# Rearranging the first two batches of a fused attention and MLP kernel: heads on partition halves, spare banks, and a new order of loads

## The chip, the core and the metric

The kernel runs on one core of one Trainium2 chip. The time is that of one launch on the device, in microseconds (us): the median of repeated runs. A second number, the span, is read from a profiled execution, from its first to its last instruction. Five engines matter: TensorE (matrix products; PE in the tables), ScalarE (ACT), VectorE (DVE), GpSimd (POOL), and SyncE (SP), which here issues most of the transfers (DMA). Matrix products write to PSUM, which this kernel divides into eight banks of 512 fp32 columns.

## What is computed

```python
def _attn_ref(q, k, v):                      # each (8 batches, 8 heads, 576 tokens, 64)
    window, dilation, scale = 32, 4, 1.0 / np.sqrt(64)
    scores = scale * np.matmul(q, k.transpose(0, 1, 3, 2))
    rel = pos[:, None] - pos[None, :]
    mask_plain = (rel >= 0) & (rel < window)
    mask_dil = (rel >= 0) & (rel < window * dilation) & (rel % dilation == 0)
    # heads 0 to 3 take mask_plain, heads 4 to 7 take mask_dil
    ...                                      # masked softmax over the keys
    return np.matmul(attn, v)

x = attn_out.transpose(0, 2, 1, 3).reshape(4608, 512)
h = x @ w_in                                 # (512, 2048)
out = np.maximum(0.01 * h, h) @ w_out        # (2048, 512)
```

All inputs and the output are fp32 in DRAM; the kernel computes in fp16 with fp32 sums.

## The kernel before

A small planner in the Python source orders every instruction of every engine before the program is emitted. Priorities (`prio`) and the tables `WHEN`, `FIRST` and `RANKS` steer it; the engines then run their lists strictly in that order.

**The first two batches.** The q and k of batches 0 and 1 (`b < EARLY`) are loaded in rows of 1 KB and turned by TensorE; batches 2 to 7 come later in another way. In each batch a visit `hp` takes two heads: visits 2 and 3 the dilated heads, 0 and 1 the plain ones. Part 0 of a visit has units 0 and 1, part 1 has unit 2, which needs the last 64 tokens ("rest").

```python
FIRST = "bbii0iiicicooii1oooooo"     # order of loads: b, c = q, k, v of batch 0, 1
                                     # i, o = 512 KB of w_in, w_out; 0, 1 = rest of a batch
def heads_of(vi):
    return 4 * (vi // 2) + vi % 2, 4 * (vi // 2) + vi % 2 + 2
...
# load_group: v of the dilated heads, twice with an overlap
lv = [load("SP", at(vs, 0, 128, i * 256, [512, 4], [1, 256]),
           dram(v, base + i * 64 * D, [4 * D, 128], [HS, 4], [1, 256]), 512, 1024, ...)
      for i in range(2)]
...
# load_rest: eight transfers of 16 partitions each
for vi in (2, 3, 0, 1):
    for o, src in ((0, q), (1, k)):
        p0 = 32 * vi + 16 * o
        lo.append(load("SP", at(st, p0, p0 + 16, 0, [256, 2], [1, 256]), ..., 32, 1024, ...))
```

**One unit.** TensorE adds a mask and the scores into one PSUM bank; ScalarE takes the exponential; TensorE multiplies by v. Beside the 64 columns of v lie 64 columns of ones, so that rows 64 to 127 of the result hold the sum of the weights. ScalarE makes the reciprocal as exp(-ln), and VectorE multiplies.

```python
sps = [bank("sps0")]                          # one bank for scores
ops = [bank(f"ops{i}") for i in range(2)]     # two for the weighted values
hps = [bank(f"hps{i}") for i in range(2)]     # two for the MLP's first product
fps = [bank(f"fps{i}") for i in range(2)]     # two for its second; fps[1] also turns k
...
nc.tensor.matmul(st[:, 0:384], ident, bias, start=True, stop=False)            # mask
nc.tensor.matmul(st[:, 192 * i:192 * i + 192], ka, qa, ...)                    # scores, x2
nc.scalar.activation(out=et, in_=st[:, 0:384], func=AF.Exp, scale=SCALE)
for hh in range(2):
    nc.tensor.matmul(ot[:, c:c + 96], va, et[:, c:c + 96], start=True, stop=True)  # x4, 128 columns of v and ones
nc.scalar.activation(out=rt, in_=ot[64:128, 0:384], func=AF.Ln)
nc.scalar.activation(out=rt, in_=rt, func=AF.Exp, scale=-1.0)
nc.vector.tensor_tensor(out=at(xt[m % 2], ...), in0=at(ot, 0, 64, ...), in1=at(rt, 0, 64, ...), op=ALU.mult)
```

**The MLP.** The 4608 tokens make 12 chunks of 384: three for each pair of batches. Chunk 0 is the first 384 tokens of batch 0, chunk 1 those of batch 1, chunk 2 the rest of both.

```python
def up(c, j, ...):        # 16 per chunk: four matmuls of 384 columns, then ACT into gt
    nc.tensor.matmul(ht[:, 0:n], w_in[:, ...j...], at(xt[m % 2], ...), start=(i == 0), stop=(i == NI - 1))
    nc.scalar.activation(out=gt[...], in_=ht[:, 0:n], func=AF.Prelu, alpha=0.01)

def down(c, tt, ...):     # 12 per chunk (3 tt of 4 parts): four matmuls of 512 columns
    nc.tensor.matmul(ft, g[:, ...j...], w_out[:, j * DM:j * DM + DM], start=(j == 0), stop=(j == NJ - 1))
```

Part p of a `down` needs w_out's blocks 4p to 4p+3, that is two of the eight transfers marked `o` in `FIRST`; an `up` needs two of the eight marked `i`.

Of the kernel before, what the change touches and what calls it, by code (L numbers as in the profile page):

```python
# [14 lines left out]
WIN = 32  # L15
AHEAD, LATE = 5.0, 4.0
WHEN = (-5.0, 15.0, 50.0, 77.0, 112.0, 138.0, 172.0, 200.0)
FIRST = "bbii0iiicicooii1oooooo"
RANKS = ((-100.0, 1.0), (-50.0, 1.0), (-40.0, 1.0), (5.0, 1.0))


def _constants():

    ident = np.eye(128, dtype=np.float16)
    p = np.arange(128)[:, None]
    key = p - 32
    c = np.arange(96)[None, :]
    qry = 4 * (c % 24) + c // 24
    rel = qry - key
    band = (rel >= 0) & (rel < WIN)  # L30
    first = band & (key >= 0)
    rel0 = c - p
    d0 = (rel0 >= 0) & (rel0 < WIN)
    c1 = np.arange(48)[None, :]
    rel1 = 96 + c1 - (16 + p)
    d1 = (rel1 >= 0) & (rel1 < WIN)
    masks = np.concatenate([first, band, band, d0, d1], axis=1)
    parts = [ident, masks, np.where(masks, 0.0, -60000.0)]
    return np.concatenate([x.astype(np.float16) for x in parts], axis=1)
# [94 lines left out]
def kernel(  # L134
# [23 lines left out]
    EARLY = 2  # L158

# [19 lines left out]
    NMASK = 288 + 96 + 48  # L179
# [3 lines left out]
    M_PL, M_D0, M_D1 = 128, 128 + 288, 128 + 288 + 96  # L183
# [12 lines left out]
    rc = [sbuf(f"rc{i}", [64, 384], FP32) for i in range(NR)]  # L196
# [3 lines left out]
    rest = sbuf("rest", [128, 512])  # L200
# [5 lines left out]
    sps = [bank("sps0")]  # L206
    ops = [bank(f"ops{i}") for i in range(2)]
    hps = [bank(f"hps{i}") for i in range(2)]
    fps = [bank(f"fps{i}") for i in range(2)]
# [7 lines left out]
    def took(n, size):  # L217
        for a, ta, b, tb in ((4, 9.0, 128, 15.0), (128, 15.0, 256, 20.0), (256, 20.0, 1024, 52.0),
                             (1024, 52.0, 2048, 92.0)):
# [4 lines left out]
    def load(queue, dst, src, n, size, deps, prio):  # L224
# [3 lines left out]
                        LATE if prio > -1478 else 0.0)  # L228
# [27 lines left out]
    for i in range(NT):  # L256
        p = (-2000 if i == 0 else -1900) + i
        t_zero[i] = ([clear("DVE", qbd[i][64:128, 0:S], 0.34, 0.0, p),
                      clear("DVE", qbd[i][0:64, S:2 * S], 0.34, 0.0, p)],
                     [clear("DVE", kt[i][:, 0:PAD], 0.1, 0.0, p)])  # L260
    t_ones = {}
    for i in range(NV):
        p = -1950 if i == 0 else -700
# [7 lines left out]
    kept = {}  # L271

    def heads_of(vi):
        return 4 * (vi // 2) + vi % 2, 4 * (vi // 2) + vi % 2 + 2

    def load_group(b, g, prio):
# [7 lines left out]
        for o, src in ((0, q), (1, k)):  # L284
# [3 lines left out]
            if first:  # L288
                lo = [load(queue, at(st, 0, 128, j * 256, [512, 2], [1, 256]),
                           dram(src, base + j * HS, [4 * D, 128], [2 * HS, 2], [1, 256]),  # L290
# [15 lines left out]
        if dil:  # L306
            lv = [load("SP", at(vs, 0, 128, i * 256, [512, 4], [1, 256]),
                       dram(v, base + i * 64 * D, [4 * D, 128], [HS, 4], [1, 256]),
                       512, 1024, v_old, prio) for i in range(2)]
        elif b == 0:  # L310
            lv = [load("SP", at(vs, PAD, 128, 0, [1, D]), dram(v, 0, [D, 96], [1, D]),
                       96, 256, v_old, prio),
                  load("SP", at(vs, 0, 128, D, [D, 23], [1, D]),
                       dram(v, 64 * D, [D, 128], [96 * D, 23], [1, D]),
                       2944, 256, v_old, prio), t_vz]
        else:
            lv = [load("SP", at(vs, 0, 128, 0, [D, 24], [1, D]),
                       dram(v, base - 32 * D, [D, 128], [96 * D, 24], [1, D]),
                       3072, 256, v_old, prio)]

        for j in range(2):
            nn, n_old = ring("NAT", NNAT, n_users := [])
            na, c_qk = nat[nn], []
            for o in range(2):
                st, s_users = stage[o]
                if early:
                    dst = at(na, 0, 128, o * 512, [D, 2], [128, 4], [1, D])
                    src = at(st, 0, 128, j * 256, [512, 2], [D, 4], [1, D])
# [9 lines left out]
            if not dil:  # L338
                c_v = [cast(at(vt, 0, 128, 0, [768, 2], [128, 6], [1, D]),
                            at(vs, 0, 128, j * 384, [768, 2], [D, 6], [1, D]), 768,  # L340
                            lv + d_old, prio)]
            elif early:
                c_v = [cast(at(vt, 0, 128, i * 512, [1024, 2], [128, 4], [1, D]),
                            at(vs, 0, 128, j * 512 + i * 256, [1024, 2], [D, 4], [1, D]), 512,
                            lv[i:i + 1] + d_old, prio) for i in range(2)]
            else:
                c_v = [cast(at(vt, 0, 128, 0, [1024, 2], [128, 8], [1, D]),
                            at(vs, 0, 128, j * 512, [1024, 2], [D, 8], [1, D]), 1024,
                            lv + d_old, prio)]
            v_users += c_v  # L350
            kept[b, 2 * g + j] = vt, d_users, c_v[1:]
            if early:
                c_v = c_v[:1]
            visits[b, 2 * g + j, 0] = (na, c_qk, n_users, vt,
                                       c_v + [t_ones["d" if dil else "p", dn]], d_users)

    def load_rest(b, prio):

        _, r_old = ring("REST", 1, r_users := [])
        sn, s_old = ring("STG", NST, s_users := [])  # L360
        st, lo = stg[sn], []
        for vi in (2, 3, 0, 1):
            for o, src in ((0, q), (1, k)):
                p0 = 32 * vi + 16 * o
                lo.append(load("SP", at(st, p0, p0 + 16, 0, [256, 2], [1, 256]),
                               dram(src, (b * H + heads_of(vi)[0]) * HS + 512 * D,
                                    [4 * D, 16], [2 * HS, 2], [1, 256]),
                               32, 1024, s_old, prio))
        c = cast(at(rest, 0, 128, 0, [D, 2], [128, 4], [1, D]),
                 at(st, 0, 128, 0, [256, 2], [D, 4], [1, D]), 512, lo + r_old, prio, CENG)  # L370
        s_users.append(c)
        for vi in range(NP):
            vt, d_users, c_v = kept[b, vi]
# [4 lines left out]
    def load_w(n, prio):  # L378
# [15 lines left out]
        for i in range(2):  # L394
            c = cast(dst[i], st[:, i * 512:i * 512 + 512], 512, [t], prio, WENG)
# [7 lines left out]
    WENG = ("POOL", "DVE")  # L403
# [17 lines left out]
    def pieces(b, dil, u):  # L421

        m, res = b // 2, []
        u_lo, u_hi = ((0, 96) if u < 2 else (96, 144)) if dil else (48 * u, 48 * u + 48)
        for u0, nu, base in segs[b]:
# [5 lines left out]
            if dil and u < 2:  # L431
                res.append((key, base + 2 * u * nu + lo - u0, [[nu, 2], [1152, 2], [1, n]], 0,
                            [[192, 2], [96, 2], [1, n]]))
            elif dil:
                res.append((key, base + lo - u0, [[nu, 4], [1152, 2], [1, n]], 0,
                            [[96, 4], [48, 2], [1, n]]))
            else:
                res += [(key, base + 1152 * hh + lo - u0, [[24, 2], [nu, 4], [1, 24]], 96 * hh,
                         [[192, 2], [24, 4], [1, 24]]) for hh in range(2)]
# [7 lines left out]
    def move(dst, src, n, deps, prio):  # L447

        def fn(e):
            if e == "ACT":  # L450
                nc.scalar.copy(out=dst, in_=src)  # L451
            else:
                nc.vector.tensor_copy(out=dst, in_=src)  # L453
        return add((("DVE", 0.1 + n * 0.00065), ("ACT", 0.06 + n * 0.00085)), None, 0.2, deps, fn,
                   prio)

    slot_of, turned_rest = {}, {}

# [7 lines left out]
    def turn(b, hp, part, prio):  # L466
# [30 lines left out]
        def turn_in(bank, src, c):  # L497
            def pe(e):
                for s in range(4):
# [4 lines left out]
        def q_to(i, lo, hi, deps):  # L504
# [5 lines left out]
            else:  # L510
                o, od, id_ = 360 + lo, [[24, 4], [1, n]], [[128, 4], [1, n]]
            return [move(at(qb, 64 * hh, 64 * hh + 64, hh * S + o, *od),
                         at(tpb, 64 * hh, 64 * hh + 64, i, *id_), 4 * n, deps + old + zq, prio)
                    for hh in range(2)]

        def k_to(bank, i, lo, hi, deps):
            n = hi - lo
            if dil:
                o, od = lo, [[144, 4], [1, n]]
            else:  # L520
                o, od = PAD + 4 * lo, [[1, 4], [4, n]]
            return [move(at(kb, 0, 128, o, *od), at(bank, 0, 128, i, [128, 4], [1, n]), 4 * n,
                         deps + old + zk, prio)]

        if part == 1:
            if hp == 2:
                _, q_old = ring("TP", 1, q_users := [])
                tq = add("PE", 0.23, 0.25, c_qk + [t_con] + q_old, turn_in(tpb, na, 0), prio, 0.2)
# [3 lines left out]
            new = (q_to(32 * hp, 128, 144, [tq]) + k_to(tpb, 32 * hp + 16, 128, 144, [tq]))  # L532
            q_users += new
            ev += new
        else:
# [3 lines left out]
            for lo, hi in ((0, 128),) if dil else ((0, 120), (120, 128)):  # L539
                q_users += q_to(lo, lo, hi, [tq])  # L540
            _, k_old = ring("TPK", 1, k_users := [])
            tk = add("PE", 0.23, 0.25, [c_qk[1], t_con] + k_old, turn_in(tpk, na, 512), prio, 0.2)
# [285 lines left out]
```

The softmax here doesn't subtract the row's maximum and nothing guards it: scores larger than these inputs give would overflow.

## Time and profile before

| | |
|---|---|
| time, median of 3 runs | 329.41 us (329.33 to 329.97) |
| span of the profiled execution | 328.3 us |
| TensorE busy | 307.8 us, 94% |
| ScalarE busy | 234.1 us, 71% |
| VectorE busy | 173.6 us, 53% |
| GpSimd busy | 115.4 us, 35% |
| moved by DMA | 52.04 MB, mean 158 GB/s |

Busy shares are averages over stages. A `down` is in the profile a group `fps<-w_out,gt`, an `up` a group `hps<-xt,w_in`. "xN" counts instructions; four make one `up` or one `down`. In tables of instructions in order of time the first number is the start, the second the length.

### The profile page before, as it was taken

Reading aid. Unit: us, or ns where it says so; the run is one execution under the profiler, and the core shown is the slowest. Engines: PE = TensorE matmul, PEld = TensorE weight load, DVE = VectorE, ACT = ScalarE, POOL = GpSimd, SP = SyncE. Lnnn points to the kernel's source line nnn. Section 1 sums busy time; section 2 is a strip of 40 time slices with the busy share of each in tenths; the row PEclk is TensorE's granted clock in tenths of the full one; section 3 lists DMA queues with packets and bytes.
Section 4 is the critical chain, followed back from the end, with each engine's and each line's share of the span. In section 5 each row is a group of like instructions: output and inputs, shape, how many; then the busy total and the mean of one; then the engine's idle time right before and its main releaser. Section 6 shows DMA issues by size and latency. Waiting matters only on the chain.

```text
span 328.3 us, 6295 instructions
## 1 busy us (share of the span) xinstructions
PE 307.8 (94%) x2238; PEld 182.3 (56%) x2238; DVE 173.6 (53%) x382; ACT 234.1 (71%) x520; POOL 115.4 (35%) x166
## 2 busy tenths in 40 slices
PE   6666988999999999999999999999999999999994
PEld 3444654556667656565555555555555555555541
DVE  7455677443777586976865867666343411000011
ACT  2787997854989799699988888887788853334300
POOL 6524443227445371772744736456000000000000
PEclk9997999999999999999999999999999999999998
DMA  8979989999999999999999999996111111111113
GB/s 241 293 239 349 301 271 310 180 228 143 214 151 219 181 156 210 143 212 202 164 189 158 235 193 150 212 166 138 32 34 32 35 32 34 47 50 34 32 32 96
DMA packets 160831, 52.04 MB, mean 158 GB/s; under 512 B 139168, under 2 KB 152096, under 8 KB 160800
## 3 DMA queue, kind: packets, MB, share of 16 engines
q1 hardware_dynamic: 160112, 50.86, 75.3%
q10 hardware_dynamic: 688, 0.78, 1.0%
q8 instruction: 17, 0.28, 0.4%
q14 instruction: 14, 0.11, 0.2%
HBM read 42.19 MB, written 9.44 MB: 157 GB/s over the span
## 4 chain that ended last, share of the span: by engine, by line
PE 78%; ACT 12%; DVE 5%; issue 3%; DVEq 0%
PE fps L706 36%; PE hps L666 34%; PE sps L592 3%; PE ops L631 3%; ACT rc L639 3%; ACT ee L598 3%; ACT gt L673 2%; ACT rc L642 2%; ACT qbd L451 1%; DVE qbd L241 1%; ACT kt L451 1%; DVE qbd L453 1%; DVE kt L453 1%; PE ops L621 1%; PE sps L573 1%
## 5 line engine op out<-in xcount | busy, mean ns | idle before, releaser
L666 PE MATMUL hps<-xt,w_in 128*128 128x384 f16 (+1 forms) x832 | 153.4, 315 | 1.8 <-ACT gt L673 1.2
L706 PE MATMUL fps<-w_out,gt 128*128 128x512 f16 x576 | 146.0, 379 | 0.0
L673 ACT ACTIVATE gt<-hps 128x384 f16<-128x384 f32 (+1 forms) x208 | 95.3, 464 | 50.2 <-PE hps L666 48.2
L666 PEld LDWEIGHTS <-w_in 128*128 128x128 f16 x832 | 76.4, 98 | 45.7 <-issue 2.6
L647 DVE TENSOR_TENSOR xt<-ops,rc 64x192 f16<-64x192 f32 (+1 forms) x144 | 56.1, 411 | 48.9 <-ACT rc L642 48.1
L706 PEld LDWEIGHTS <-gt 128*128 128x128 f16 x576 | 54.5, 98 | 46.7 <-issue 0.4
L715 DVE COPY osb<-fps 128x512 f32<-128x512 f32 x36 | 24.7, 685 | 60.1 <-PE fps L706 59.0
L487 POOL COPY qbd<-turned 64x576 f16<-64x576 f16 x48 | 34.1, 710 | 59.6 <-DVE turned L482 51.4
L598 ACT ACTIVATE ee<-sps 128x384 f16<-128x384 f32 x96 | 46.8, 488 | 9.4 <-PE sps L592 7.6
L639 ACT ACTIVATE rc<-ops 64x384 f32<-64x384 f32 x96 | 46.7, 487 | 8.9 <-PE ops L631 5.0
L612 DVE TENSOR_TENSOR ee<-ee,con 128x384 f16<-128x384 f16 x72 | 35.4, 492 | 29.0 <-ACT ee L598 28.3
L642 ACT ACTIVATE rc<-rc 64x384 f32<-64x384 f32 x96 | 49.6, 518 | 1.6
L237 POOL CAST nat<-stg 128x576 f16<-128x576 f32 (+1 forms) x55 | 36.0, 678 | 23.8 <-DMA stg<-in_q_dram 15.6
L592 PE MATMUL sps<-qbd,kt 128*128 128x192 f16 x160 | 26.5, 247 | 1.4 <-ACT kt L451 0.7
L592 PEld LDWEIGHTS <-kt 128*128 128x128 f16 x160 | 16.0, 103 | 19.6 <-issue 7.2
L493 DVE STREAM_TRANSPOSE kt<-nat 128x576 f16<-128x576 f16 x24 | 18.0, 763 | 3.7 <-POOL nat L237 3.5
L482 DVE STREAM_TRANSPOSE turned<-nat 128x576 f16<-128x576 f16 x24 | 18.0, 762 | 0.1
L631 PEld LDWEIGHTS <-vp 128*128 128x128 f16 x192 | 12.9, 98 | 8.8 <-issue 2.0
L237 POOL CAST vd<-vst 128x1024 f16<-128x1024 f32 (+1 forms) x20 | 17.0, 881 | 1.9 <-DMA vst<-in_v_dram 1.7
L631 PE MATMUL ops<-ee,vp 128*128 128x96 f16 x192 | 15.9, 206 | 1.1 <-DVE xt L647 1.0
L237 POOL CAST vp<-vst 128x768 f16<-128x768 f32 x16 | 13.4, 862 | 6.6 <-DMA vst<-in_v_dram 6.3
L573 PE MATMUL sps<-con 128*128 128x384 f16 x24 | 7.9, 331 | 6.1 <-ACT ee L598 5.9
(49 smaller groups left out, 130.1 us busy)
## 6 DMA issues: line engine op xcount, KB each, us to landing
vst<-in_v_dram SPq DMA_DIRECT2D x16, 512.0 KB, 6.2
stg<-in_q_dram SPq DMA_DIRECT2D x48, 144.0 KB, 4.8
stg<-in_k_dram SPq DMA_DIRECT2D x48, 144.0 KB, 4.3
vst<-in_v_dram SPq DMA_DIRECT2D x7, 768.0 KB, 6.8
out_dram<-osb SPq DMA_DIRECT2D x16, 192.0 KB, 2.9
gt<-in_moe_w_in_dram SPq DMA_DIRECT2D x5, 512.0 KB, 6.8
out_dram<-osb SPq DMA_DIRECT2D x24, 96.0 KB, 2.1
out_dram<-osb SPq DMA_DIRECT2D x16, 128.0 KB, 2.9
```

The lines of the kernel that those rows point to most:

```text
L237: ENG[e].tensor_copy(out=dst, in_=src)
L487: lambda e, p0=p0, hh=hh: nc.gpsimd.tensor_copy(out=at(qb, p0, p0 + 64, hh * S + o, *od), in_=at(xb, p0, p0 + 64, i, *id_)), prio)
L592: nc.tensor.matmul(st[:, 192 * i:192 * i + 192], ka, qa, start=not by_pe, stop=i == 1 or not by_pe)
L598: lambda e: nc.scalar.activation(out=et, in_=st[:, 0:384], func=AF.Exp, scale=SCALE), prio + 0.1)
L612: ENG[e].tensor_tensor(out=io, in0=io, in1=mk, op=ALU.mult)
L631: nc.tensor.matmul(ot[:, c:c + 96], va, et[:, c:c + 96], start=True, stop=True)
L639: lambda e: nc.scalar.activation(out=rt, in_=ot[64:128, 0:384], func=AF.Ln),
L642: lambda e: nc.scalar.activation(out=rt, in_=rt, func=AF.Exp, scale=-1.0),
L647: nc.vector.tensor_tensor(out=at(xt[m % 2], h0 % 2 * 64, h0 % 2 * 64 + 64, h0 // 2 * 1152 + x, *o_), in0=at(ot, 0, 64, c, *i_), in1=at(rt, ...
L666: nc.tensor.matmul(ht[:, 0:n], w_in[:, i * DFF + j * 128:i * DFF + j * 128 + 128], at(xt[m % 2], 0, 128, i * 1152 + x0 + x, [1, n]), start ...
L673: lambda e: nc.scalar.activation(out=gt[c % NG][:, j * n_c + x:j * n_c + x + n], in_=ht[:, 0:n], func=AF.Prelu, alpha=0.01),
L706: nc.tensor.matmul(ft, g[:, j * n_c + tt * 128:j * n_c + tt * 128 + 128], w_out[:, j * DM:j * DM + DM], start=(j == 0), stop=(j == NJ - 1))
```

## The change

It touches batches 0 and 1 only, and the order of the loads.

- A unit's two heads now lie next to each other in the model's width, and their weighted values are written to partitions 0 to 63 and 64 to 127 of one bank, by matmuls of 64 columns; two more matmuls with a tile of ones write the sums beside them. Ln, Exp and the final product then work on 128 partitions by 192 columns, where it was 64 by 384.
- In batch 0's part 0, before the MLP needs them, one `hps` bank serves as a second bank for scores and the other as a third for weighted values.
- The last 64 tokens of q and k come in two transfers of 128 partitions, where it was eight of 16. The dilated v is loaded once; its last 64 tokens follow in a small transfer.
- The turned k is copied out with a contiguous destination; in batch 1, q and k are turned into one bank. Most of these copies are now VectorE's alone.
- The loads come in a new order, with weights ahead of most of batch 1, and v apart from q and k.

```diff
-FIRST = "bbii0iiicicooii1oooooo"
-RANKS = ((-100.0, 1.0), (-50.0, 1.0), (-40.0, 1.0), (5.0, 1.0))
+FIRST = "ibvbv0iiooiicioiicyoooooy1"          # v, y: v of batch 0, 1
+RANKS = ((-40.0, 2.0), (5.0, 0.5), (-40.0, 1.0), (40.0, 3.0))
...
-    sps = [bank("sps0")]
+    banks = {"S": [bank("sps0")], "O": ops}
+    banks["S0"] = banks["S"] + hps[1:]
+    banks["O0"] = ops + hps[:1]
...
+    return (2 * vi, 2 * vi + 1) if b < EARLY else (4 * (vi // 2) + vi % 2, ...)
...
+        if dil and early:
+            lv = [load("SP", at(vs, 0, 128, 0, [256, 4], [1, 256]),
+                       dram(v, base, [4 * D, 128], [HS, 4], [1, 256]), 512, 1024, v_old, prio_v)]
...
+        for o, src in ((0, q), (1, k)):
+            lo.append(load("SP", at(st, 0, 128, o * 256, [1, 256]),
+                           dram(src, b * H * HS + 512 * D, [HS, 8], [4 * D, 16], [1, 256]),
+                           128, 1024, s_old, prio))
+        lv = load("SP", at(vs, 0, 16, 1024, [256, 4], [1, 256]), ..., 64, 1024, v_old, prio)
...
-                o, od = PAD + 4 * lo, [[1, 4], [4, n]]                         # k_to
+                o, od, id_ = PAD + 4 * lo, [[4, n], [1, 4]], [[1, n], [128, 4]]
...
+            if tiled:                                                          # values
+                for x in range(5 if small else 3):
+                    for hh in range(2):
+                        p0 = 64 * hh
+                        if x == (4 if small else 2):
+                            nc.tensor.matmul(ot[p0:p0 + 64, 192:384], ones, ...)
+                        ...
+                            nc.tensor.matmul(ot[p0:p0 + 64, 96 * x:96 * x + 96],
+                                at(vt, 0, 128, (...) * 128, [1, D]), et[...], ...)
...
+        if tiled:
+            r_in, r_out, n_r = ot[:, 192:384], rt[:, 0:192], 192
...
-                down(n_c, tt, acts, gt_free[n_c])
+                end = tt * 128 + 128
+                down(n_c, tt, [[t for t, x in a if x < end] for a in acts], gt_free[n_c])
```

Matmuls on idle data that keep TensorE busy in the gaps are put in by the planner up to the first `down`, before and after.

## The prediction

> **What bounds the kernel now.** I read the stages first: busy time in five stretches of the span. The columns are the stretch, its length, then busy time and instructions of PE, PEld, DVE, ACT and POOL, the granted TensorE clock, the DMA share and GB/s.
>
> ```profile
> 0.00:30.00 30.00, 18.86 (x166) 11.93 (x167) 16.82 (x58) 20.15 (x44) 14.36 (x26) 0.99 0.95 273
> 30.00:57.75 27.75, 24.09 (x200) 15.09 (x198) 19.31 (x48) 24.45 (x57) 11.70 (x18) 0.95 0.98 301
> 57.75:75.00 17.25, 17.25 (x121) 9.85 (x120) 7.32 (x17) 11.89 (x26) 5.25 (x8) 1.00 1.08 195
> 75.00:323.50 248.50, 247.64 (x1756) 145.38 (x1754) 129.52 (x260) 177.57 (x395) 84.05 (x116) 1.00 0.71 128
> ```
>
> From 57.75 us to the last product at 323.5 us TensorE is busy for 264.9 of 265.75 us. What happens there can't be shortened by making another engine faster. Before 57.75 us it is another kernel: the DMA share is 0.95 to 0.98, and TensorE's busy time holds waits, fillers and a slow clock. So the question is how much of the MLP is done when the packed part begins. TensorE's instructions in order of time show it:
>
> ```profile
> 29.99 1.49 PE L666 MATMUL hps<-xt,w_in 128*128 128x384 f16 x4
> ...
> 50.55 1.13 PE L706 MATMUL fps<-w_out,gt 128*128 128x512 f16 x4
> ...
> 57.75 1.46 PE L666 MATMUL hps<-xt,w_in 128*128 128x384 f16 x8 [0.99 <-ACT gt L673]
> ```
>
> The first up runs at 30 us, the first down at 50.6, and the up at 57.75 is the first of chunk 1. By the order of instructions, 16 ups and 2 downs lie before it; 10 downs of chunk 0 are still owed. Why so late, GpSimd's list tells, since its casts start when data lands (the bracket is the idle time before, and what ended it):
>
> ```profile
> 16.72 1.60 POOL L237 CAST vp<-vst 128x768 f16<-128x768 f32 x2 [2.76 <-DMA vst<-in_v_dram]
> 19.59 0.61 POOL L237 CAST w_in<-gt 128x512 f16<-128x512 f32 x1 [1.26 <-DMA gt<-in_moe_w_in_dram]
> 24.68 0.61 POOL L237 CAST w_in<-wst 128x512 f16<-128x512 f32 x1 [4.49 <-DMA wst<-in_moe_w_in_dram]
> ...
> 36.78 0.61 POOL L237 CAST nat<-stg 128x512 f16<-128x512 f32 x1 [0.98 <-DMA stg<-in_q_dram]
> ...
> 42.03 1.79 POOL L237 CAST vp<-vst 128x768 f16<-128x768 f32 x2 [3.03 <-DMA vst<-in_v_dram]
> ...
> 61.90 0.67 POOL L237 CAST w_out<-xt 128x512 f16<-128x512 f32 x1 [1.90 <-DMA xt<-in_moe_w_out_dram]
> ```
>
> The last weights land at 61.9 us, so chunk 0 can't be finished before. The rates of the transfers over the first 75 us, in 40 slices of 1.875 us, say whether the memory was at its limit:
>
> ```profile
> GB/s 7 187 382 348 348 348 311 218 274 388 115 121 283 357 310 377 351 364 359 334 235 239 378 318 369 90 54 368 380 342 334 286 89 149 138 139 113 308 359 151
> ```
>
> Some 350 GB/s is the usual rate; the dips to 115 and 121 (20 to 24 us) and to 90 and 54 (47 to 51 us) are the sixteen small rest transfers. Inside the early units ScalarE is the engine that is waited for:
>
> ```profile
> PE sps L573 <- ACT ee L598: 5.9, 9, 1.2
> ```
>
> ```profile
> L642 ACT ACTIVATE rc<-rc 64x384 f32<-64x384 f32 x24 | 12.3, 517 | 0.2
> L639 ACT ACTIVATE rc<-ops 64x384 f32<-64x384 f32 x24 | 11.6, 486 | 1.2 <-PE ops L631 0.6
> ```
>
> Nine times the single score bank waited for the exponential, 5.9 us in all; Ln and Exp of the sums take about 1.0 us for each of 24 units.
>
> **What the Trainium skill says.** "ScalarE: Activation LUTs", section "What ACT_TABLE_LOAD costs", gives 186 ns + 0.833 ns per element for an activation with immediates: 506 ns for 384 columns, where the trace has 486 and 517. For 192 columns it gives an estimate of 346 ns. "DMA: Bandwidth & Descriptors", section "Measured (HBM→SBUF, 128 partitions, SWDGE, issued from GpSimd)", calls transfers under 64 KB dominated by their descriptors; the eight of 32 KB here agree (worked out below). "TensorEngine Tiling (Array Packing)", sections "Key Properties" and "Restrictions", says that column tiles can work at once, that a change of mode drains the array, and that tiling turns off the fast weight load; nothing in this trace shows any of it. "TensorE: Matmul & The Clock Gate", "Part 1", says that an idle window of about 3.4 us halves the clock. The trace agrees: the first up, after a stretch of fillers and waits, takes 1.49 us where later ones are 0.65 apart.
>
> **The parts.** *Tiled units.* ScalarE loses 2 x (0.50 - 0.35) = 0.3 us a unit, 24 units: 7 us. VectorE: 128x192 once (0.35, as 64x192 has now) in place of 0.55 or of two at 0.34: about 6 us in all. TensorE: four products of 96 columns and two of 192 are 768 columns where it was 384; at 0.163 us for 384 (a quarter of an up) that is +0.16 us a unit or +4 us in all if nothing runs side by side, but nearly all of it before the packed part. *Spare banks.* They serve 8 of 24 units and can take up to some 4 of the 5.9 us of waits. *Contiguous k.* The plain k copies cost 1.2 to 1.3 us against 0.41 for the dilated; I expect 0.4 to 0.7, four times. These three make batch 0 ready sooner: its first up should run at 23 to 25 us in place of 30. None of them shortens the end by itself, since weights land later than that.
>
> *Loads.* This is the part that counts. Eight transfers of 512 KB between 24.68 and 36.78 us give 1.51 us each. The plain v, 768 KB in rows of 256 bytes, took 42.03 - 36.78 - 1.51 = 3.7 us. The eight rest transfers and one of weights took 24.68 - 19.59 = 5.1, so the rest took 3.6 us for 256 KB. In the new kernel a first w_in (+512 KB) and a dilated v loaded once (-512 KB) cancel out: batch 0's plain v lands at 16.7 again. The rest, two transfers of 128 KB and one of 64 KB, I take as 1.1 us: 17.8. Twenty transfers of 512 KB follow in the list before batch 1's plain v. I find no buffer in their waits that isn't long free, so at 1.51 us: the last w_in, the 12th, at 35.9; the last w_out, the 20th, at 48.0 (61.9 before); batch 1's plain v at 51.7 (42.0 before); its rest at 52.5 to 52.8.
>
> *TensorE's new order.* Before the first up of chunk 1 stand 16 ups and 12 downs: all of chunk 0. After the last w_out only some six downs and the units are left, 6 x 0.865 = 5.2 us, which fits into 48.6 to 54. What decides then is batch 1's tail: rest q, k at 52.5, cast of twice the columns 1.0, turning 0.7, two final products 0.35 each and four copies of 0.19 on VectorE 1.5 with a handover of 0.2, mask and scores 0.6, exponential 0.75, values 0.7, all with their handovers: 58.0 us for chunk 1's first up, as late as before.
>
> *Sum.* The packed part was 265.75 us with 10 downs owed; without them it is 265.75 - 10 x 0.865 = 257.1. The units left then are a little fewer (-0.5). The span is 58.0 + 257.1 - 0.5 + the end after the last product, 4.8 = 319.4. I add 1.0 for a slow clock or holes, because fillers now end with the first down at about 31 us while TensorE still waits for w_out between 36 and 48. The median lies 329.41 - 328.3 = 1.1 above the span: 321.5 us.
>
> **Rivals.** *(a) Loads run as now planned but less densely:* a wait on a buffer, or GpSimd behind (it casts alone all of w_in, 16 x 0.61 us, and the turned inputs wait in its list), moves everything after it. Against: 14 casts between 25.6 and 39 us are only 8.5 us. Each microsecond is one in the result; 3 us late gives 324.5. *(b) The array suffers:* mode changes around the 64-column products and slow clock from 36 us on. If each tiled unit cost 0.3 us more than I count, the 12 of batch 1 give 3.6 us, partly in waiting time: 323 to 325. *(c) ScalarE becomes the limit in chunk 1,* since ups now come without the downs of chunk 0 between them and only two `hps` banks hold them: 16 activations of 0.47 and about 4.5 us of units are 12 us against some 15 us of TensorE. So I expect no hole, or 1 us. Likewise batch 2 is needed some 8 us sooner; its loads start about as before, at 53, and its first scores come near 75, so 2 us at most. *(d) Only the unit's shortening counts, and the loads were hidden:* then downs would still come late, and the time stays at 327 to 329. Against it stands the DMA share of 0.95 to 0.98. *(e) Better:* the units of batch 1 finish faster than my chain, at 55 to 56: 318 to 319.5.
>
> **Range and chances.** The memory sets a floor near 52 us for batch 1, so the gain hardly passes 11 us; (a) and (b) pull the other way, one at a time some 3 us, seldom both. I put eight tenths in 317.5 to 327.0. Two per cent faster is 322.8, just above my number: 0.62; within 2%, 0.33; slower, 0.05, for a stall that the order doesn't show.
>
> **What would show it.** Right: the last w_out cast starts near 48, the plain v of batch 1 is cast near 52, no dip for the rest, first up at 23 to 25, first down near 31, all 12 downs of chunk 0 before the up of chunk 1 at 57 to 59, and TensorE full from there on. Ln and Exp near 350 ns. Wrong: the up of chunk 1 after 60, holes of several us in TensorE after it, or values products far above 0.33 us a unit.

## The result, and the profile after

| | before | after |
|---|---|---|
| time, median | 329.69 us (329.33 to 330.18) | 320.99 us (320.75 to 322.0) |
| ratio | | 0.974, 95% interval 0.9715 to 0.9767 |
| span of the profiled execution | 328.3 us | 319.4 us |
| first up of chunk 0 | 29.99 us | 24.56 us |
| first up of chunk 1 | 57.75 us, two downs done | 58.14 us, all twelve done |
| last w_out cast by GpSimd | 61.90 us | 47.09 us |

The kernel is 8.7 us faster. The busy time by stretch of the kernel after, with the columns as in the prediction (the last stretch ends at the last product, 314.5 us):

```profile
0.00:30.00 30.00, 23.72 (x217) 14.78 (x218) 20.71 (x73) 15.97 (x41) 17.14 (x32) 0.94 0.97 308
30.00:57.75 27.75, 25.35 (x212) 14.44 (x210) 19.11 (x54) 14.45 (x39) 14.99 (x21) 1.00 1.00 301
57.75:75.00 17.25, 17.19 (x132) 10.34 (x133) 5.08 (x13) 11.32 (x28) 7.40 (x10) 1.00 1.07 217
75.00:314.50 239.50, 239.06 (x1714) 140.96 (x1711) 124.88 (x257) 174.63 (x393) 78.83 (x108) 1.00 0.58 123
```

TensorE is full from 57.75 us on, as it was before. ScalarE has lost 14.2 us of busy time in the first 57.75 (20.15 + 24.45 before, 15.97 + 14.45 now). TensorE's instructions in order of time, for the first up, the first down, and the first up of chunk 1 with what stands just before it:

```profile
24.56 0.33 PE L741 MATMUL hps<-xt,w_in 128*128 128x384 f16 x1
...
32.30 1.04 PE L782 MATMUL fps<-w_out,gt 128*128 128x512 f16 x4
...
57.81 0.31 PE L678 MATMUL ops<-ee,vd 128*64 128x48 f16 x8 [1.56 <-DVE xt L722]
57.93 0.28 PE L672 MATMUL ops<-ee,ones 128*64 128x192 f16 x2
58.14 1.47 PE L741 MATMUL hps<-xt,w_in 128*128 128x384 f16 x8
```

GpSimd's casts show when the last weights and batch 1's plain v land:

```profile
47.09 0.62 POOL L243 CAST w_out<-xt 128x512 f16<-128x512 f32 x1 [0.57 <-DMA xt<-in_moe_w_out_dram]
...
49.63 0.83 POOL L243 CAST vp<-vst 128x768 f16<-128x768 f32 x1 [1.92 <-DMA vst<-in_v_dram]
```

And the rate of the transfers over the first 75 us, in slices of 1.875 us:

```profile
GB/s 3 227 278 383 385 385 327 287 245 211 252 364 403 376 399 403 404 381 381 384 401 407 398 360 306 120 189 166 244 178 168 169 230 387 214 77 182 195 240 266
```

Where the rests are loaded (15 to 21 us, 50 to 54 us) the rate falls to 211 and 166, no longer to 115 and 54. The one slice of 120 lies at 47 to 49 us, ahead of the rest. The groups of the early units, by shape (count, busy us, mean ns, idle time before):

```profile
L718 ACT ACTIVATE rc<-rc 128x192 f32<-128x192 f32 x23 | 7.7, 365 | 0.3
L722 DVE TENSOR_TENSOR xt<-ops,rc 128x192 f16<-128x192 f32 x21 | 7.0, 350 | 9.3 <-ACT rc L718 9.1
L716 ACT ACTIVATE rc<-ops 128x192 f32<-128x192 f32 x21 | 6.4, 329 | 8.7 <-PE ops L672 8.7
```

Ln and Exp take 329 and 365 ns, where it was 486 and 517. The waits for the exponential, 5.9 us before, no longer appear among TensorE's longest waits.

### The profile page after: what moved, and what is told of

It is laid out like the page before. It is cut to its first block, busy times and chain, and to the rows that moved or that the text cites. A ratio compares the mean times of both kernels' runs of the same rounds, so it can differ in the third digit from the quotient of the medians.

```text
span 319.4 us, 6338 instructions
## 1 busy us (share of the span) xinstructions
PE 305.7 (96%) x2270; PEld 180.5 (57%) x2270; DVE 170.5 (53%) x396; ACT 216.4 (68%) x499; POOL 118.4 (37%) x170
## 2 busy tenths in 40 slices
DMA packets 159711, 51.14 MB, mean 160 GB/s; under 512 B 138944, under 2 KB 150848, under 8 KB 159680
## 4 chain that ended last, share of the span: by engine, by line
PE 85%; ACT 5%; DVE 5%; DMA 2%; issue 2%; SPq 0%; DVEq 0%
PE fps L782 37%; PE hps L741 36%; PE sps L642 4%; PE ops L704 3%; DMA stg<-in_q_dram 2%; DVE qbd L479 2%; ACT gt L748 2%; ACT ee L648 1%; ACT rc L716 1%; ACT rc L718 1%; PE tp L527 1%; DVE kt L479 1%; PE sps L623 1%; DVE xt L722 1%; PE ops L694 1%
## 5 line engine op out<-in xcount | busy, mean ns | idle before, releaser
L741 PE MATMUL hps<-xt,w_in 128*128 128x384 f16 (+1 forms) x832 | 150.6, 314 | 0.6 <-DVE xt L722 0.4
L722 DVE TENSOR_TENSOR xt<-ops,rc 64x192 f16<-64x192 f32 (+2 forms) x130 | 49.3, 401 | 39.1 <-ACT rc L718 37.8
L648 ACT ACTIVATE ee<-sps 128x384 f16<-128x384 f32 x92 | 44.7, 485 | 13.4 <-PE sps L642 12.4
L662 DVE TENSOR_TENSOR ee<-ee,con 128x384 f16<-128x384 f16 x72 | 33.6, 467 | 33.6 <-ACT ee L648 33.1
L716 ACT ACTIVATE rc<-ops 64x384 f32<-64x384 f32 (+1 forms) x94 | 41.6, 450 | 14.7 <-PE ops L672 8.7
L718 ACT ACTIVATE rc<-rc 64x384 f32<-64x384 f32 (+1 forms) x96 | 45.1, 479 | 1.6
L243 POOL CAST vd<-vst 128x1024 f16<-128x1024 f32 (+2 forms) x16 | 15.4, 980 | 5.2 <-DMA vst<-in_v_dram 4.0
L704 PEld LDWEIGHTS <-vp 128*128 128x128 f16 x144 | 10.0, 98 | 6.1 <-issue 0.5
L243 POOL CAST vp<-vst 128x768 f16<-128x768 f32 x14 | 11.3, 829 | 4.3 <-DMA vst<-in_v_dram 4.1
L479 DVE COPY qbd<-tp 64x64 f16<-64x64 f16 (+3 forms) x40 | 10.9, 274 | 3.2 <-PE tp L527 2.4
L704 PE MATMUL ops<-ee,vp 128*128 128x96 f16 x144 | 12.0, 206 | 0.2 <-DVE ee L662 0.2
```

The costliest lines, as they stand in the source:

```text
L243: ENG[e].tensor_copy(out=dst, in_=src)
L648: lambda e: nc.scalar.activation(out=et, in_=st[:, 0:384], func=AF.Exp, scale=SCALE), prio + 0.1)
L662: ENG[e].tensor_tensor(out=io, in0=io, in1=mk, op=ALU.mult)
L716: lambda e: nc.scalar.activation(out=r_out, in_=r_in, func=AF.Ln), prio + 0.2)
L718: lambda e: nc.scalar.activation(out=r_out, in_=r_out, func=AF.Exp, scale=-1.0),
L722: nc.vector.tensor_tensor(out=dst, in0=at(ot, p0, p1, c, *i_), in1=at(rt, p0, p1, c, *i_), op=ALU.mult)
```

## The experiments

Two numbers carry most of the readings below: the start of chunk 0's first up, when batch 0 is ready, and the start of chunk 1's first up with the downs done by then. The prediction's sum turns the second into the span: start + 265.75 - 0.865 x (downs done - 2) + 4.8. For the changed kernel it gives 58.14 + 265.75 - 8.65 + 4.8 = 320.0; measured 319.4. In all runs it holds within 1.2 us. Chunk 1's first up is the seventeenth up of TensorE's list in each of them. Each run was timed beside the kernel before on the same chip; "gain" below is the difference of these two medians. The changed kernel's is 8.7 us, and an interval of a ratio is mostly some 0.9 us to either side, 1.9 in e1.

### e1: the old order of loads

```diff
-FIRST = "ibvbv0iiooiicioiicyoooooy1"
-RANKS = ((-40.0, 2.0), (5.0, 0.5), (-40.0, 1.0), (40.0, 3.0))
+FIRST = "bvbvii0iiicyicyooii1oooooo"
+RANKS = ((-100.0, 1.0), (-50.0, 1.0), (-40.0, 1.0), (5.0, 1.0))
```

> The new kernel with the old order of loads and the old priorities; units, banks, transfers and copies stay new. By its list of instructions 2 downs stand before the first up of chunk 1, as before the change. Theory L (what counts is how much of chunk 0 is done when the packed part begins, and the order of loads decides that): most of the gain goes; smaller transfers still end the loads some 6 us sooner than before, so chunk 1 may begin at 54: 54 + 265.8 + 4.8 + 1.1 = 325.7, between 324 and 328. Theory U (shorter units on ScalarE and VectorE make the gain): near the new kernel, 321 to 322.5.

Measured: 320.76 us (319.68 to 324.27), ratio 0.975 (0.969 to 0.981), gain 8.75 us: as fast as with the new order. The profiled execution is the slowest of the four (324.27 us, span 321.3); the other three took 319.68 to 320.99, with spans of 317.6 to 318.9. In it the last w_out is cast at 56.95 us, and at chunk 1's first up only two downs are done:

```profile
46.79 1.03 PE L527 MATMUL tp<-con,rest 128*128 128x128 f16 x8 [0.85 <-DVE rest L243]
47.62 2.70 PE L741 MATMUL hps<-xt,w_in 128*128 128x384 f16 x8
...
50.49 1.46 PE L741 MATMUL hps<-xt,w_in 128*128 128x384 f16 x8
```

By the order of the instructions the two ups at 47.62 are still chunk 0's; of the two at 50.49 the first is chunk 0's last, and the second, at 51.14, is chunk 1's first. Ten owed downs cost 8.65 us, and chunk 1 starts 7.0 us sooner than in the changed kernel; by the sum this execution ends 1.65 us later, and its span is 1.9 longer. A half-speed stretch is part of that: the granted clock is 0.50 from 46.7 to 50.1 us, and two ups take 2.70 us where 1.46 is usual. The three faster executions were not profiled; from their spans the sum gives a start of chunk 1 at 47 to 48.4 us (an estimate). The theory that the order makes the gain falls here, by the times.

### e2: the old units with the new order

```diff
-FIRST = "bbii0iiicicooii1oooooo"                      # the kernel before
+FIRST = "ibb0iiooiicioiicooooo1"                      # and RANKS of the changed kernel
```

> The kernel before with the new order of loads and the new priorities only; v stays with q and k, units stay old. By its list 6 downs stand before the first up of chunk 1. Theory L: 4 downs fewer are owed, 3.5 us; small rest transfers and the v loaded twice still cost bandwidth, so chunk 1 begins no sooner: 325 to 327.5. Theory U: no gain, 329 to 330, or a loss since ScalarE has no more room than before.

Measured: 333.27 us (331.75 to 333.92), ratio 1.0105 (1.0074 to 1.0135), 3.8 us slower than the kernel before: the order by itself, on the old units and loads, is a loss. First up at 31.07 us, chunk 1's at 61.25 with six downs done. TensorE waits for the exponential even more often than before:

```profile
PE sps L573 <- ACT ee L598: 7.6, 12, 1.2
```

### e3: the old layout of units in the changed kernel

```diff
-    TILED = (0, 1)
+    TILED = ()                # and the ones beside v again; the rest of the change is kept
```

> The new kernel with the units as before: values and ones in one product of 128 columns, Ln and Exp on 64 partitions by 384, one or two products on VectorE. All else stays new; 12 downs before chunk 1. ScalarE gets some 7 us more work in the first 58 us, where it was busy for 30.4 us; four of the 24 units lie in the chain behind the last loads, where each costs 0.3 us more on ScalarE and VectorE each. Theory L: 321.5 to 323. Theory U: 325 or more.

Measured: 323.57 us (322.57 to 324.71), ratio 0.982 (0.979 to 0.985), gain 5.9 us: the tiled units are worth 2.8. Ln and Exp are back at 484 and 516 ns, and the first up slips from 24.56 to 27.80:

```profile
27.80 0.33 PE L741 MATMUL hps<-xt,w_in 128*128 128x384 f16 x1
...
61.19 2.76 PE L741 MATMUL hps<-xt,w_in 128*128 128x384 f16 x8
```

The last w_out, meanwhile, is cast at 46.57 us, a little earlier than in the changed kernel. So no weight was late; batch 0 was, by 3.2 us, and chunk 1 is late by 3.05. In between the delay is smaller: the last down of chunk 0 runs at 56.18, 1.85 later than in the changed kernel, and the other 1.2 us come with batch 1's old units after it. (The 2.76 us are ups at half speed: the granted clock is 0.50 from 60.5 to 64.0 us.)

### e4: one more megabyte

```diff
+        if n in (3, 4, 5, 6):     # a load of 256 KB ahead of each of four w_in; its data is not used
+            load("SP", (osb + [spare])[n - 3], dram(moe_w_out, 0, [DM, 128], [1, DM]), 128, 2048, [], prio)
```

> The new kernel with four loads of 256 KB more, which nothing uses, among the loads of w_in. In the new kernel's trace 512 KB took some 1.36 us, so 1 MB takes 2.7 us. Theory L (the memory sets when batch 1 and the last weights are there): +2.5 to +3 us, 323.5 to 324. If the loads had slack, or the units set the pace: within 0.5 us of the new kernel.

Measured: 323.69 us (323.07 to 324.5), ratio 0.9815 (0.979 to 0.983), gain 5.8 us. 1 MB costs 2.9 us; at the 390 GB/s of these microseconds it needs 2.7. First up 26.15, chunk 1's 61.16. Bytes in this stretch count in full; the dilated v, loaded once and without its overlap in each of two batches, saves 0.90 MB of them (52.04 MB moved before, 51.14 after), and by this run I estimate its share at some 2.5 us; it wasn't undone by itself.

### e5: no spare banks

```diff
-    banks["S0"] = banks["S"] + hps[1:]
-    banks["O0"] = ops + hps[:1]
+    banks["S0"] = banks["S"]
+    banks["O0"] = ops
```

> The new kernel without the spare banks: batch 0's part 0 has one bank for scores and two for values, as before the change. The run with the old order of loads took Theory L away: order alone gains nothing. Theory S (many small parts, each shortening the way through batches 0 and 1, add up): the waits of the score bank come back for 8 units, +0.5 to +2 us. Theory M (memory traffic alone, fewer and better transfers): within 0.5 us of the new kernel.

Measured: 320.53 us (320.49 to 322.17), ratio 0.971 (0.969 to 0.974), gain 9.6 us: nothing is lost without them. The first up comes even a little earlier (23.95 us).

### e6: the rest in eight transfers

```diff
-            lo.append(load(..., dram(src, b * H * HS + 512 * D, [HS, 8], [4 * D, 16], [1, 256]), 128, 1024, ...))
+            for h in range(0, 8, 2):
+                lo.append(load("SP", at(st, 16 * h, 16 * h + 32, o * 256, [1, 256]),
+                               dram(src, (b * H + h) * HS + 512 * D, [HS, 2], [4 * D, 16], [1, 256]), 32, 1024, ...))
```

> The new kernel with the last 64 tokens of q and k in eight transfers of 32 KB on 32 partitions each, per batch, where it has two of 128 KB on 128. Before the change the sixteen small ones brought the memory down to 50 to 120 GB/s for some 3.6 us each time. Theory M: +2.5 us for each batch, up to +5 us. Theory S: +1 to +3 us, as part of the sum. If only the width in partitions mattered, less, since these have 32 in place of 16.

Measured: 328.19 us (326.54 to 330.32), ratio 0.994 (0.991 to 0.996), gain 1.9 us: 6.8 of the 8.7 are gone. The rate of the transfers:

```profile
GB/s 9 242 254 380 379 386 330 263 60 45 215 240 233 375 392 387 400 405 405 371 385 383 404 410 390 359 275 111 48 79 175 213 173 179 192 185 290 305 98 186
```

At 15 to 19 us and at 51 to 56 us it is 45 to 111 GB/s: the dips of the kernel before are back. In a view of single microseconds the DMA share from 16 to 19 us is 0.12 to 0.22, so the sixteen DMA engines had too little to do. SyncE's list shows why (start, length of the issue):

```profile
7.90 7.21 SPq L233 DMA_DIRECT2D stg<-in_q_dram  x4
15.15 2.56 SPq L233 DMA_DIRECT2D stg<-in_k_dram  x4
...
18.21 0.43 SPq L233 DMA_DIRECT2D gt<-in_moe_w_in_dram  x1
```

Four transfers of 32 KB take 2.56 us to issue, 0.64 each, that is 51 GB/s and no more, and the weights behind them are issued at 18.21. In the changed kernel the same transfer of weights is issued 3.7 us earlier:

```profile
14.49 0.42 SPq L233 DMA_DIRECT2D gt<-in_moe_w_in_dram  x1
```

That the issuing limits the rate is my reading of these lines; no run tests it alone. In the kernel before, with 16 partitions a transfer, most of the first eight took 0.42 us to issue, and the rate fell all the same (115 and 121 GB/s). The first up comes at 28.20 us, 3.6 later; the last w_out at 50.10, 3.0 later; batch 1's rest is cast at 57.64 where it was 51.92, and chunk 1's first up is at 63.13. That is 5.0 us later, where the medians differ by 6.8: the profiled execution, 326.73 us, is one of the faster of ten. The six of 327.59 us and more had mean granted clocks of 0.975 to 0.984, the other four 0.989 to 0.993; none of the six was profiled.

### e7: the plain k copied out with a stride

```diff
-                o, od, id_ = PAD + 4 * lo, [[4, n], [1, 4]], [[1, n], [128, 4]]
+                o, od, id_ = PAD + 4 * lo, [[1, 4], [4, n]], [[128, 4], [1, n]]
```

> The new kernel with the plain k copied as before the change, strided in the destination. Four copies: in the new kernel's trace a plain k takes 0.51 to 0.57 us, before 1.1 to 1.3. Theory S: +0.5 to +1.5 us, since two of the four stand in batch 0's way and VectorE alone carries batch 1's. Theory M: within 0.5 us.

Measured: 324.36 us (324.07 to 324.69), ratio 0.982 (0.980 to 0.983), gain 5.8 us: 2.9 us for the four copies, and for the small plain k copies of the rests, which the edit also turns back (0.30 us where it was 0.22). VectorE's list shows the plain copies at 1.30 us, where the changed kernel has 0.69 (the 0.51 to 0.57 expected were means over plain copies and dilated ones of 0.42):

```profile
44.90 1.30 DVE L479 COPY kt<-tp 128x512 f16<-128x512 f16 x1
...
49.28 1.31 DVE L479 COPY kt<-tp 128x512 f16<-128x512 f16 x1
...
55.45 1.15 DVE L243 CAST rest<-stg 128x1024 f16<-128x1024 f32 x1
```

The last line is the telling one. The last w_out is cast at 46.76 us, as early as in the changed kernel, and the last tokens of v at 51.41; but VectorE comes to the cast of the rest only at 55.45, where it was:

```profile
51.92 0.69 DVE L243 CAST rest<-stg 128x1024 f16<-128x1024 f32 x1
```

The loads were in time. The engines' lists, which run strictly in order, were late since batch 0: first up 27.26, chunk 1's 61.23. TensorE's list is here the changed kernel's, instruction by instruction, and it runs 2.35 us behind it from the second to the sixteenth up and 3.0 to 3.1 behind it from the third down to chunk 1.

### e8: one half after the other

```diff
-                for x in range(5 if small else 3):
-                    for hh in range(2):
+                for hh in range(2):
+                    for x in range(5 if small else 3):
```

> The new kernel with each unit's products sorted by half: all of partitions 0 to 63 first, then all of 64 to 127. Same instructions, other order. In the new kernel two units stand 0.19 us apart, though their 768 columns at an up's pace would take 0.33. If products on different halves run beside each other only when they alternate, a unit goes to 0.28 to 0.33 us, and the time by 24 x 0.1 = 2.4 us at most, less where TensorE waits anyway: +0 to +2 us. If the order doesn't matter: no change.

Measured: 321.96 us (321.71 to 324.59), ratio 0.976 (0.972 to 0.980), gain 8.2 us. The order of the halves hardly matters, and even so they run side by side. Two units of this kernel in TensorE's list:

```profile
52.99 0.28 PE L684 MATMUL ops<-ee,vp 128*64 128x96 f16 x4
...
53.18 0.26 PE L684 MATMUL ops<-ee,vp 128*64 128x96 f16 x4
```

The second begins 0.19 us after the first. A unit's 768 columns in a row would take 0.33. In the changed kernel the pair stands at 52.55 and 52.74; its second unit and what follows:

```profile
52.74 0.25 PE L684 MATMUL ops<-ee,vp 128*64 128x96 f16 x4
52.82 0.25 PE L672 MATMUL ops<-ee,ones 128*64 128x192 f16 x2
53.01 1.04 PE L782 MATMUL fps<-w_out,gt 128*128 128x512 f16 x4
```

So 0.19 us is a unit that another tiled one follows. Ahead of a product of full width it takes 0.27 to 0.29 in the changed kernel (0.27 to 0.30 here), and a third unit of the dilated heads, with eight products of 48 columns, 0.33 (0.36 to 0.39 here). A unit of the kernel before takes 0.17 to 0.20.

### e9: the old order and the rest in eight transfers

The edits of e1 and e6 together.

> The changed kernel with the old order of loads (as in e1, 320.8 us) and, besides, the rest of q and k in eight small transfers again (as in e6, which lost 7.2 us). Theory B, bytes and rates: in either order the memory is the limit until batch 1 is complete, so the time lost on small transfers is lost at the end whatever the order; about 320.8 + 7 = 327 to 329 us. Rival: the order decides how much the rest's slowness hurts. In the old order fewer weights stand after the rest of batch 1, TensorE has downs of chunk 0 to fill the hole with once w_out lands, and the loss is at most half: 322 to 325 us. If the loss is larger (over 330), the new order is worth something after all, as a protection against slow rests.

Measured: 327.08 us (324.97 to 328.11), ratio 0.991 (0.988 to 0.994), gain 2.8 us. The rest in eight transfers costs 8.75 - 2.8 = 6.0 us here and 6.8 in the new order. Chunk 1's first up is at 55.13 with two downs done, in e1 at 51.14; the wait that leads the list is for the rest:

```profile
PE tp L528 <- DVE rest L243: 4.9, 2, 2.5
```

### e10: a third order

```diff
-FIRST = "ibvbv0iiooiicioiicyoooooy1"
+FIRST = "ibvbv0iiiiiicyicyo1ooooooo"      # and w_out's 4th to 6th transfer staged in gt[2], not gt[1]
```

> The changed kernel with a third order: all of w_in ahead of batch 1, one transfer of w_out between batch 1's plain q, k and its rest, the other seven of w_out last; three of those are staged in another buffer (chunk 2's instead of chunk 1's), so that chunk 1's ups don't wait for them. Theory B: a transfer of weights moved from before batch 1 to after it brings chunk 1's first up 1.4 us earlier and leaves 1.5 downs (1.3 us) owed, so any order is worth the same within some 2 us: first up of chunk 1 near 45 to 46 with no downs done, a sum of 45.5 + 265.75 + 1.7 + 4.8 = 317.8 us for the span without holes, and 318 to 321.5 us for the time. Rival: the first theory of the prediction, that downs owed are a loss: chunk 1 would start hardly sooner than in e1 and the time be 323 to 328 us.

Measured: 322.48 us (322.18 to 323.06), ratio 0.9775 (0.974 to 0.981), gain 7.4 us. The time is near the others', but not by the way I expected: chunk 1's first up is at 52.72 us with six downs done, not at 45 with none, although batch 1's rest is cast at 43.6. VectorE is busy 10.08 of the 11 us from 42 to 53, and from the first up to chunk 1's TensorE is busy 26.70 of 27.94, fillers included (columns as above):

```profile
24.78:52.72 27.94, 26.70 (x235) 15.39 (x234) 19.36 (x61) 19.06 (x49) 14.71 (x24) 1.00 1.00 327
42.00:53.00 11.00, 10.20 (x82) 5.23 (x81) 10.08 (x35) 5.35 (x15) 5.14 (x8) 1.00 0.96 315
```

### e11: contiguous k alone, in the kernel before

```diff
-                o, od = PAD + 4 * lo, [[1, 4], [4, n]]
+                o, od, id_ = PAD + 4 * lo, [[4, n], [1, 4]], [[1, n], [128, 4]]
```

> The kernel before with one part of the change alone: the plain k is copied out with a contiguous destination. Theory B: the four copies at 1.2 to 1.3 us fall to 0.6 to 0.7, on the chain that makes a batch ready; undone in the changed kernel they cost 3.4 us. In the kernel before, chunk 1's first up waits for batch 1's chain too, so 2 to 3 us come: 326.5 to 327.5 us. Rival: in the kernel before the weights that land at 61.9 us and the small rests hide it, and the time stays within 0.7 us of 329.7.

Measured: 329.74 us (328.85 to 331.43), ratio 1.000 (0.9975 to 1.0024). What is worth 2.9 us in the changed kernel is worth nothing here; my first theory was wrong. The casts after batch 1's plain q and k show why:

```profile
38.93 0.64 POOL L237 CAST nat<-stg 128x512 f16<-128x512 f32 x1 [1.00 <-DMA stg<-in_k_dram]
...
48.90 0.61 POOL L237 CAST w_in<-xt 128x512 f16<-128x512 f32 x1 [1.27 <-DMA xt<-in_moe_w_in_dram]
50.82 0.61 POOL L237 CAST rest<-stg 128x512 f16<-128x512 f32 x1 [1.30 <-DMA stg<-in_k_dram]
```

The plain k is there at 39 us, the last w_in at 49, and the rest at 50.8: a copy that is 0.6 us shorter ends in the same wait.

### e12: less for VectorE, in the third order

```diff
-            c = cast(dst[i], st[...], 512, [t], prio, ("POOL",) if n < 8 else CENG)     # CENG: GpSimd, VectorE
+            c = cast(dst[i], st[...], 512, [t], prio, ("POOL",) if n < 8 else ("POOL", "ACT"))
```

> The kernel of e10 (third order, 322.5 us; chunk 1's first up at 52.72 us with six downs done, although the rest of batch 1 was cast at 43.6) with one change: of each 512 KB of w_out the second half is cast by ScalarE and not by VectorE (eight casts, 3.7 us of VectorE's list between 42.9 and 53.8 us). Theory V: with the weights out of the way, VectorE's list is what sets the end of batch 1 (10.1 us busy of the 11 from 42 to 53), so the final products and the copies of the rest come up to 3 us sooner: chunk 1's first up at 49.5 to 51 us with four or five downs done; by the sum, 50.3 + 265.75 - 2.5 x 0.865 + 4.8 = 318.7 us for the span and 320 to 321 us for the time. Theory B alone (bytes decide): the loads are the same, and the time stays at 322 to 323 us. A third way: ScalarE's casts stand ahead of Exp and Ln in its list and delay the units; then it is 323 us or more.

Measured: 321.42 us (320.62 to 322.79), ratio 0.974 (0.971 to 0.976), gain 8.6 us against e10's 7.4; the intervals overlap. In the profiled execution batch 0 was ready later than in e10 (first up 26.23 against 24.78), and chunk 1's first up, at 53.99 with five downs done, comes 27.8 us after it, in e10 27.9. VectorE still has 9.42 of 11 us. That VectorE's list sets this stretch is not shown. No version beats the changed kernel beyond the spread; e1, e5 and e12 equal it.

## Why the prediction was right, and where it was not

**The time and the sum.** 321.5 was said, 320.99 measured. The last w_out was to start near 48.0 (47.09), batch 1's plain v near 52 (GpSimd takes its half at 49.63, VectorE at 51.45), the rest at 52.5 (51.92), the first up at 23 to 25 (24.56), the first down near 31 (32.30), chunk 1's first up at 58.0 after twelve downs (58.14), the span at 319.4 (319.4). The 1.0 us for slow clock and holes wasn't needed: the clock is 1.00 from 30 us on. The median stands 1.6 us above the span, not 1.1. No rival was needed: (a) and (c) show no hole, and (b) is refuted, since no tiled unit takes more than 0.33 us. (d) is refuted by the time; its thought that the units' shortening counts was right in part (e3). A slip without effect: the first dip of the rate lies at 18.75 to 22.5 us, not at 20 to 24.

Luck has a part in 58.0. It was reckoned from the landing of batch 1's rest; but in e5, where batch 1's last loads come no earlier (the plain v is cast at 49.62, the last tokens of v at 51.98, in the changed kernel at 49.63 and 51.93), chunk 1 starts 0.6 us sooner, and in e7, with the loads in time, 3.1 later. The start followed the engines' lists. Later loads delay it too (e4, e6), so the two limits lie close together in the changed kernel, and the chain that I reckoned ended at the same moment.

**The step that failed** is the attribution: "*Loads.* This is the part that counts", and of the three small parts, "None of them shortens the end by itself, since weights land later than that." Both halves are wrong. The order, undone, costs nothing (e1), and put into the kernel before it costs 3.8 us (e2). The ten owed downs are real, but they are paid for by a later start of chunk 1 (7.0 us in e1's profiled execution, by the sum some ten in its faster ones), since the weights now stand before batch 1's loads. I compared 58.0 with 57.75 and took the late start of the kernel before as a property of its order; it was one of its slow rests and units. In the old order chunk 1 starts at 57.75 with both, at 55.13 with the slow rests alone (e9) and at 51.14 with neither (e1).

The small parts do shorten the end. The table sets the two starts beside each other, all in the new order with twelve downs between:

| | first up | chunk 1's first up | apart |
|---|---|---|---|
| changed kernel | 24.56 | 58.14 | 33.6 |
| e3, old units | 27.80 | 61.19 | 33.4 |
| e5, no spare banks | 23.95 | 57.58 | 33.6 |
| e7, strided k | 27.26 | 61.23 | 34.0 |
| e8, halves in turn | 24.93 | 58.62 | 33.7 |
| e4, 1 MB more | 26.15 | 61.16 | 35.0 |
| e6, rest in eight | 28.20 | 63.13 | 34.9 |

From the first up on, TensorE's list holds 16 ups, 12 downs and batch 1's units, and takes some 33.5 us; slower loads add about 1.4 (e4, e6). In the changed kernel TensorE is busy for 30.73 us of it (columns as above):

```profile
24.56:58.14 33.58, 30.73 (x266) 17.54 (x266) 21.77 (x63) 18.73 (x50) 18.34 (x27) 1.00 1.01 314
```

So little time is free in which a delay could be made up. In e3 and e7 the last weights land as early as in the changed kernel, and chunk 1 still starts about as much later as batch 0 was late; in e7 the delay can be followed through the whole list, in e3 a part of it comes anew with batch 1. A microsecond on batch 0's way to its first up is thus about one at chunk 1's start, though no run delays batch 0 alone. The kernel before, counted with twelve downs, had 29.99 to the first up and 57.75 - 29.99 + 10 x 0.865 = 36.4 from there. So of the gain 5.4 us lie before the first up and 36.4 - 33.6 = 2.8 after it, 8.2 together; the span shrank by 8.9. A half-speed stretch of the kernel before is part of the 2.8: its granted clock is 0.50 from 29.2 to 32.6 us, which I estimate at 1.3 us at most (half of the 2.6 us from its first up on).

**Part by part.** *Rest transfers:* 3.6 us was to become 1.1, twice, 5 us in all. Nearly right in size (6.8 in e6, 6.0 in e9), and it counts under loads, as said, but not through the new order: this is the largest single part, and in e6 the delay shows both before the first up (3.6) and in batch 1 (1.3 more). *Tiled units:* 7 us of ScalarE were to be saved and 14.2 were (copies moved to VectorE are part of that); TensorE was to pay up to 0.33 us a unit and pays 0.19 to 0.33. Worth 2.8 us at the end, not none. *Contiguous k:* 0.69 us, at the top of the 0.4 to 0.7 said; worth 2.9, not none. *Spare banks:* "up to some 4 of the 5.9 us of waits"; worth nothing (e5). Without the banks TensorE waits 0.6 us in all for the exponential in e5. *Order:* nothing (e1). Not undone by themselves: the single load of the dilated v, the turning of batch 1's q and k into one bank, and new engines for casts (all of w_in by GpSimd, early v by GpSimd or VectorE).

**Why the parts don't add up.** Undone one at a time they give 6.8 + 2.9 + 2.8 + some 2.5 for the v = 15.0, against 8.7 in all. e9 and e11 show the reason: while the rest comes late, the work behind it hides in its wait. In the old order, units, banks, k and v together bring 2.8 us; the wide rests on top of them 6.0 more. Each part's value holds with the others in place. The third order gains nothing from its earlier loads: counted with twelve downs, e10 takes 27.94 + 6 x 0.865 = 33.1 us from its first up and e12 27.8 + 7 x 0.865 = 33.8, like the changed kernel, and TensorE is busy for most of that. Which engine sets what waits remain is open.

## What to carry to other kernels

Work still owed at a point (ten downs) and the time at which that point is reached belong into one sum: moving one load ahead of another changes both, and here the two cancel within 1 us in the medians. Look first for stretches where the DMA share and the rate fall together (e6: a share of 0.12 to 0.22, 45 to 60 GB/s), since they delay everything that stands behind them in strictly ordered lists, and expect the parts hidden behind such a stretch to show no gain until it is gone. Whether a part is off the path is told by undoing it, not by a later landing of something else.

## What the runs showed of the hardware

- Eight transfers of 32 KB on 32 partitions in a row held the rate at 45 to 60 GB/s for some 4 us, with larger loads behind them in the same list; four of them took 0.64 us each to issue (e6). Two of 128 KB on 128 partitions left it at 211 to 252 in the changed kernel. "DMA: Bandwidth & Descriptors", as quoted in the prediction, puts the cost of small transfers on descriptors; here the pace of issuing fits the numbers as well.
- The 64-column products on two partition halves ran side by side: 768 columns in 0.19 us, in either order of issue, where another tiled unit follows. "TensorEngine Tiling (Array Packing)", "Key Properties", says that tiles work in parallel, and this agrees. It also names a drain at a change of mode; ahead of a full-width product a unit takes 0.08 to 0.10 us more, but no run tells a drain from the next weight load (98 ns). A weight load of 64 columns takes 108 to 110 ns.
- A copy of 512 fp16 elements from PSUM to SBUF took 1.30 us on VectorE with a destination stride of 8 bytes and a contiguous source, 0.69 with a contiguous destination and a source stride of 256 bytes (ScalarE: 1.30 and 0.59). The copies of the dilated k, contiguous on both sides in runs of 128, took 0.42. The Trainium skill's "SBUF — State Buffer", section "Door 1: The DMA port swizzle", has strides of up to 8 bf16 as free; here a stride of four fp16 in the destination was not, and the measurement decides.
- In e1 TensorE fell to half speed at 46.7 us, after 3.41 us (as long as the slow stretch itself, 46.7 to 50.1) in which it was busy for 1.85 and waited at most 0.85 at a time. In the changed kernel it was also busy for 1.85 of the 3.41 us before 58.14, waited 1.56 at a time, and kept its full clock. "TensorE: Matmul & The Clock Gate", "Part 1", names an idle window of about 3.4 us; no stretch that long was idle here. Nor was one in the kernel before, whose slow first up the prediction took for agreement: TensorE was busy for 1.48 of the 3.41 us before its clock fell at 29.2, and waited at most 1.15.
